# The kv products of a later batch in one run of 48 instead of two runs of 24

## Chip, cores, metric

The kernel runs on one core of a Trainium2 chip. The metric is device time in microseconds (us). Every profile holds one execution and is some 1.8 us shorter than the time of that execution, because it counts from the first to the last instruction.

## The reference

```python
def _attn_ref(q, k, v, g_norm):            # q, k, v: 8 batches, 8 heads, 576 tokens, 64
    kv = np.einsum('bhsd,bhse->bhde', k, v)     # one 64x64 matrix per head
    out = np.einsum('bhsd,bhde->bhse', q, kv)
    rms = np.sqrt(np.mean(out * out, axis=-1, keepdims=True) + 1e-06)
    return (out / rms * g_norm).astype(np.float32)

def _moe_ref(x, w_a, w_b, w_out):          # x: 4608 x 512, d_ff = 1536
    a = x @ w_a
    b = x @ w_b
    return (a * b @ w_out).astype(np.float32)
```

The attention output, with heads side by side, is the `x` of the second part. The kernel works in bf16 with float32 accumulation.

## The kernel before

The 4608 tokens are nine strips of 512. A strip has 12 "units", each with four products with `wa_t` and four with `wb_t` (128x128 weights, 512 columns), then four groups of 12 products with `wo_t`. Into strip s = 1 to 6 the attention of batch s + 1 is woven: `slot` runs after each unit n.

```python
def kv(self, p, o):                        # one pair of heads: 12 small products
    for c in range(EC):                    # EC = 6
        for j in range(2):
            nc.tensor.matmul(
                o[j * D : (j + 1) * D, :],                     # 64 partitions of the output
                lhsT=kt[self.b % NB][:, 2 * p + j, c, :],      # weights: 96 rows x 64 columns
                rhs=vt[self.b % NB][:, 2 * p + j, c, :],       # 64 columns to stream
                start=(c == 0), stop=(c == EC - 1))

def kv_out(self, src):                     # two casts, PSUM to SBUF, on ScalarE
    for j in range(2):
        r = slice(j * D, (j + 1) * D)
        nc.scalar.copy(kvb[self.b % 2][r, :, r], src[r])

def slot(A, s, n):
    kb = P[:, 7, 0 : NP * D].rearrange("q (p e) -> q p e", e=D)       # NP = 4
    k0, kn, xs = (4, 1, (6, 9, 11, 13)) if s < 3 else (1, 2, (4, 7, 10, 12))
    if k0 <= n < k0 + kn:
        for p in range((n - k0) * NP // kn, (n - k0 + 1) * NP // kn):
            A.kv(p, kb[:, p, :])
        if n == k0 + kn - 1:
            A.kv_out(kb)
    for p in range(NP):
        if n == xs[p]:
            A.x(p, X[0])          # two products, 128x128 weights, 288 columns
            A.psq(p, X[0])
        # ... (one unit later: two products with `ones`, reciprocal root, scaling)

for s in range(1, N_STRIP - 1):
    # ...
    for n in range(FC + 4):
        # ... (a unit, or from n = 12 on a group of output products)
        if A:
            slot(A, s, n)
        # ... (at n = 8: transpose and loads for later batches)
```

A "run" below is a stretch of small products between two 512-column products. Batches 2 and 3 (strips 1 and 2) already have one run of 48. Batches 4 to 7 (strips 3 to 6) have two runs of 24, after units 1 and 2.

## Time and profile before

| | before |
|---|---|
| time, median of three fast runs | 325.0 us (324.96 to 325.02) |
| the profiled run | 854.88 us, slow |
| TensorE busy in that profile | 98% |
| 512-column product, mean distance of starts there | 587 ns |

The profiled run was in another state than the timed ones. These are lines of its page: the span, the busy time of each engine, the chain of waits by engine, and two groups (busy us and mean ns of one after the first bar).

```profile
span 853.1 us, 4818 instructions
...
PE 835.1 (98%) x1922; PEld 267.5 (31%) x1957; DVE 124.7 (15%) x215; ACT 126.0 (15%) x212; POOL 60.4 (7%) x82
...
PE 96%; issue 2%; DMA 1%; POOL 0%; DVE 0%; ACT 0%; POOLq 0%
...
L234 PE MATMUL P<-xt,wb_t 128*128 128x512 bf16 x422 | 279.8, 834 | 3.4 <-issue 3.4
...
L250 DVE TENSOR_TENSOR ab<-P,asb 128x512 bf16<-128x512 f32 x108 | 74.7, 692 | 493.6 <-PE P L234 481.3
```

TensorE is busy throughout, and the chain is 96% TensorE. The next lines are the TensorE timeline of the same profile around the two runs of strip 5 (start, us from the first start to the last end, engine, line, operation, output and inputs, shapes, count).

```profile
497.00 2.65 PE L234 MATMUL P<-xt,wa_t 128*128 128x512 bf16 x4
499.35 2.65 PE L234 MATMUL P<-xt,wb_t 128*128 128x512 bf16 x4
501.92 0.94 PE L137 MATMUL P<-vt,kt 96*64 96x64 bf16 x24
502.80 0.68 PE L234 MATMUL P<-xt,wa_t 128*128 128x512 bf16 x1
503.80 1.41 PE L234 MATMUL P<-xt,wa_t 128*128 128x512 bf16 x2 [0.32 <-issue]
505.04 2.65 PE L234 MATMUL P<-xt,wb_t 128*128 128x512 bf16 x4
507.62 0.95 PE L137 MATMUL P<-vt,kt 96*64 96x64 bf16 x24
508.50 2.41 PE L234 MATMUL P<-xt,wa_t 128*128 128x512 bf16 x4
510.74 2.65 PE L234 MATMUL P<-xt,wb_t 128*128 128x512 bf16 x4
513.09 0.79 PE L234 MATMUL P<-xt,wa_t 128*128 128x512 bf16 x1
```

Reading it: starts are what to count, not ends, since products overlap. The step from 510.74 to 513.09 is 2.35 us for four products, 587 ns each. The group at 502.80 shows one product and the next two: one of four records is missing. From 497.00, where unit 1 begins, to 513.09, where unit 4 does, it is 16.09 us. Three plain units of 4.763 us take 14.29, so two runs of 24 cost 1.80 us here. The 48-product runs of strips 1 and 2 cost 1.726 us by the same count.

### The profile page before, as it was taken

The page shows a single profiled execution, that of the slowest core. Times are in us where ns is not written, and L with a number is a line of the kernel's source. Part 1 is how long each engine was busy: PE and PEld are TensorE (multiplying, and loading weights), DVE is VectorE, ACT ScalarE, POOL GpSimd, SP SyncE. Part 2 cuts the span into 40 slices and gives each one's busy share as a digit, 9 for nine tenths or more (in the row PEclk, how much of TensorE's full clock was granted, in tenths as well). Part 3 has the DMA queues.
Part 4 walks back from the last instruction along what each step waited for, and adds up shares of the span by engine and source line. Part 5 has one row for each costly group of instructions (what it writes and reads, how often), then busy time and mean ns, then how long its engine had stood idle before and what let it go on. Part 6 is the DMA issues. An engine that isn't in the chain of part 4 may idle for free.

```text
span 853.1 us, 4818 instructions
## 1 busy us (share of the span) xinstructions
PE 835.1 (98%) x1922; PEld 267.5 (31%) x1957; DVE 124.7 (15%) x215; ACT 126.0 (15%) x212; POOL 60.4 (7%) x82
## 2 busy tenths in 40 slices
PE   9999999999999999999999999999999999999998
PEld 3222333333233333333333333333333322222323
DVE  2211111111112011111111101110111011101110
ACT  2211111110122012111121011210211111001100
POOL 7610001000220020000200000000000000000000
DMA  9990028001990063002800010000000000010001
GB/s 190 197 106 0 25 53 84 0 0 38 124 111 0 25 79 57 0 13 65 85 0 0 38 40 1 0 25 26 0 0 13 37 0 0 13 37 0 1 12 37
DMA packets 70043, 32.61 MB, mean 38 GB/s; under 512 B 43652, under 2 KB 65540, under 8 KB 70020
## 3 DMA queue, kind: packets, MB, share of 16 engines
q0 software_dynamic: 49712, 18.44, 18.3%
q1 hardware_dynamic: 19952, 13.50, 5.9%
q10 hardware_dynamic: 356, 0.36, 0.2%
q8 instruction: 15, 0.25, 0.1%
q14 instruction: 8, 0.07, 0.0%
HBM read 37.75 MB, written 12.98 MB: 59 GB/s over the span
## 4 chain that ended last, share of the span: by engine, by line
PE 96%; issue 2%; DMA 1%; POOL 0%; DVE 0%; ACT 0%; POOLq 0%
PE P L234 59%; PE P L278 30%; PE P L188 3%; PE P L214 2%; PE P L137 2%; DMA qt<-in_q_dram 1%; DMA wb_t<-in_moe_w_b_dram 1%; PE P L175 1%; PE P L161 0%; PE P L303 0%; POOL wa_t L331 0%; POOL vt L96 0%; DVE osb L473 0%; POOL ident masks.py:199 0%; ACT osb L471 0%
## 5 line engine op out<-in xcount | busy, mean ns | idle before, releaser
L234 PE MATMUL P<-xt,wb_t 128*128 128x512 bf16 x422 | 279.8, 834 | 3.4 <-issue 3.4
L234 PE MATMUL P<-xt,wa_t 128*128 128x512 bf16 x419 | 277.6, 834 | 5.2 <-issue 5.2
L278 PE MATMUL P<-wo_t,ab 128*128 128x512 bf16 (+1 forms) x434 | 258.9, 817 | 3.6 <-issue 3.6
L250 DVE TENSOR_TENSOR ab<-P,asb 128x512 bf16<-128x512 f32 x108 | 74.7, 692 | 493.6 <-PE P L234 481.3
L234 PEld LDWEIGHTS <-wb_t 128*128 128x128 bf16 x432 | 73.9, 171 | 181.6 <-issue 181.1
L278 PEld LDWEIGHTS <-ab 128*128 128x128 bf16 x444 | 77.0, 174 | 166.1 <-issue 163.2
L234 PEld LDWEIGHTS <-wa_t 128*128 128x128 bf16 x432 | 74.7, 175 | 156.0 <-issue 155.2
L248 ACT CAST asb<-P 128x512 bf16<-128x512 f32 x108 | 63.2, 585 | 344.7 <-PE P L234 340.6
L202 DVE SCALAR_TENSOR_TENSOR xt<-P,g_col,rs 128x288 bf16<-128x288 f32 x64 | 30.2, 513 | 67.0 <-ACT rs L192 67.0
L192 ACT ACTIVATE rs<-P,eps_t 128x576 f32<-128x576 f32 (+1 forms) x33 | 24.0, 726 | 89.9 <-PE P L188 82.6
L291 ACT COPY osb<-P 128x512 f32<-128x512 f32 x17 | 9.9, 585 | 157.2 <-PE P L278 157.2
L184 ACT ACTIVATE sq<-P 128x576 bf16<-128x576 f32 x31 | 20.2, 650 | 81.2 <-PE P L214 72.6
L293 DVE COPY osb<-P 128x512 f32<-128x512 f32 x18 | 12.4, 691 | 132.5 <-PE P L278 132.5
L188 PE MATMUL P<-sq,ones 128*128 128x288 bf16 x64 | 29.8, 582 | 0.0
L116 POOL COPY gate<-qT 1x1 bf16<-1x1 bf16 x5 | 0.9, 176 | 337.9 <-DMA qT<-qs 337.9
L214 PE MATMUL P<-qT,kvb 128*128 128x288 bf16 x48 | 21.9, 579 | 0.0
L119 POOL DMA_DIRECT2D qs<-in_q_dram x12 | 19.6, 1633 | 1.8 <-issue 1.7
L188 PEld LDWEIGHTS <-ones 128*128 128x128 bf16 x64 | 11.2, 175 | 24.7 <-issue 24.7
L137 PEld LDWEIGHTS <-kt 96*64 96x64 bf16 x384 | 14.3, 169 | 14.5 <-issue 14.0
L137 PE MATMUL P<-vt,kt 96*64 96x64 bf16 x384 | 16.1, 262 | 0.9 <-DMA wb_t<-in_moe_w_b_dram 0.5
L214 PEld LDWEIGHTS <-kvb 128*128 128x128 bf16 x48 | 8.8, 183 | 19.9 <-issue 19.9
L303 PE MATMUL P<-zeros 128*128 128x512 bf16 x21 | 13.2, 773 | 1.2 <-DVE eps_t L318 1.2
(43 smaller groups left out, 78.3 us busy)
## 6 DMA issues: line engine op xcount, KB each, us to landing
out_dram<-osb SPq DMA_DIRECT2D x23, 256.0 KB, 2.0
qs<-in_q_dram POOLq DMA_DIRECT2D x12, 288.0 KB, 6.5
kt<-in_k_dram POOLq DMA_DIRECT2D x6, 576.0 KB, 9.0
vt<-in_v_dram POOLq DMA_DIRECT2D x6, 576.0 KB, 11.2
out_dram<-osb SPq DMA_DIRECT2D x13, 128.0 KB, 2.3
wo_t<-in_moe_w_out_dram POOLq DMA_DIRECT2D x12, 128.0 KB, 6.0
wa_t<-in_moe_w_a_dram POOLq DMA_DIRECT2D x5, 256.0 KB, 9.0
wb_t<-in_moe_w_b_dram POOLq DMA_DIRECT2D x5, 256.0 KB, 9.6
```

Source lines behind the costliest of these rows:

```text
L119: nc.gpsimd.dma_start(out=d[:, hs, :], in_=q[b, hs].rearrange("h t d -> t h d"))
L137: nc.tensor.matmul(o[j * D : (j + 1) * D, :], lhsT=kt[self.b % NB][:, 2 * p + j, c, :], rhs=vt[self.b % NB][:, 2 * p + j, c, :], start=(c ...
L184: nc.scalar.activation(sq[p % 3], P[:, i0 : i0 + 2, 0:HF], AF.Square)
L188: nc.tensor.matmul(P[:, i0 + h, 0:HF], lhsT=ones, rhs=sq[p % 3][:, h, :], start=True, stop=True)
L192: nc.scalar.activation(rs[p % 3][:, h0:h1, :], P[:, i0 + h0 : i0 + h1, 0:HF], AF.Abs_reciprocal_sqrt, bias=eps_t,)
L202: nc.vector.scalar_tensor_tensor(out=xt[p][:, t0 : t0 + HF], in0=P[:, x0 + h, 0:HF], scalar=g_col, in1=rs[p % 3][:, h, :], op0=ALU.mult, o ...
L214: nc.tensor.matmul(P[:, i0 + h, 0:HF], lhsT=kvb[self.b % 2][:, p, :], rhs=self.qT[:, p, h * HF : (h + 1) * HF], start=True, stop=True,)
L234: nc.tensor.matmul(self.a if w is wa_t else self.b, lhsT=w[:, kc, self.fc * 128 : (self.fc + 1) * 128], rhs=xt[kc][:, t0 : t0 + STRIP], st ...
L248: nc.scalar.copy(self.t, self.a)
L250: nc.vector.tensor_mul(abt[self.s % 2][self.fc], self.b, self.t)
L278: nc.tensor.matmul(P[:, i, e0:e1], lhsT=abt[s % 2][fc][:, g * 128 : (g + 1) * 128], rhs=wo_t[:, fc, e0:e1], start=(fc == 0), stop=(fc == F ...
L303: nc.tensor.matmul(P[:, i, 0:cols], lhsT=zeros[:, 0:128], rhs=zeros[:, 0:cols], start=True, stop=True)
```

## The change

The intent is to enter and leave the small products once per batch instead of twice, at equal work.

```diff
-        k0, kn, xs = (4, 1, (6, 9, 11, 13)) if s < 3 else (1, 2, (4, 7, 10, 12))
+        k0, kn, xs = (4, 1, (6, 9, 11, 13)) if s < 3 else (2, 1, (4, 7, 10, 12))
```

For strips 3 to 6 all four head pairs now run after unit 2. Nothing else moves on any engine.

## The prediction

> **What bounds it now.** TensorE. The page gives PE busy 98% of the span, DVE 15%, ACT 15%, POOL 7%; the chain of waits is 96% PE, and two lines alone, the a/b products and the output products, hold 89% of it. But the profiled run took 853 us against 325 us timed. In the timeline a 128x512 product starts every 587 ns on average (485, 621, 621, 621), while DVE and ACT instructions look normal (0.69 us and 0.59 us for 128x512). So only TensorE is slow in this profile, although its granted clock reads 1.00, and PE durations cannot be carried over one to one. The Trainium skill (TensorE: Matmul & The Clock Gate, Back-to-back issue gap) gives 215.7 ns for N=512 at full clock; the trace does not show that state. Estimate with it: 1296 such products (432 each with wa, wb and wo) take 279.5 us. With the smaller products and about 11 us of start-up, little of 325 us is left for stalls: the timed run is TensorE-bound too.
>
> **What the change does.** For batches 4 to 7 (strips 3 to 6) the 48 kv products (96x64 by 96x64) ran as 24 after unit 1 and 24 after unit 2; now all 48 follow unit 2. Instruction counts, the two kvb casts (0.37 us each, still after unit 2), loads and the x products' positions (from unit 4) are unchanged. Removed: four entries into and exits out of a run of small products. Nothing is added.
>
> **Cost of a run, from the raw order of starts.** Plain units take 4.763 us on average.
> - Batches 2 and 3 already have one run of 48: the two units around it take 11.253 and 11.252 us, 1.726 us more than two plain ones.
> - Batches 4 to 7 have two runs of 24: the three units around them take 16.084, 16.083, 16.089, 16.094 us, 1.80 us more than three plain ones.
>
> So one run instead of two saves about 0.07 us per batch in this slow state, 0.28 us in all; the products themselves cost about 36 ns each however grouped. At full clock the saving may differ. The skill (TensorEngine Tiling (Array Packing), Key Properties) says that changing the tiling mode drains TensorE. The slow trace shows little of such a drain, 34 to 68 ns a run; I allow 0.03 to 0.25 us per removed run, 0.1 to 1.0 us in all. All of it lies on the critical path.
>
> **Waits that could eat it.** The casts have unit 3 to hide behind before unit 4's x, as before. Bank 7 was last read for unit 13 of the strip before. k and v of batch 4 land at 232.9 and 236.7 us, 21 us after the transpose before them was issued; a strip in the timed run takes about 35 us, so they are early.
>
> **Prediction:** 324.6 us, 80% range 323.9 to 325.1. Faster by over 2%: 0.01; within 2%: 0.98; slower by over 2%: 0.01.
>
> **Right or wrong in the profile.** Right: the same instruction counts per line; one group of 48 kv products in strips 3 to 6; if it is again the slow state, units 1 to 3 together 16.0 us rather than 16.09; x products not preceded by idle PE. Wrong: PE idle before or after the run of 48, or a unit after it that waits for the a-copy or the multiply.
>
> **What would make it wrong.** A full-clock boundary cost far from the slow state's; a clock that reacts to a longer stretch of small products; 48 small products outrunning instruction supply and so costing more each than 24.

## The result

| | before | after |
|---|---|---|
| median, us | 325.01 (324.96 to 325.46, 4 runs) | 323.93 (323.9 to 324.1, 4 runs) |
| ratio after/before | | 0.9965, 95% interval 0.9947 to 0.9982 |

A ratio is the mean time of one kernel's fast runs over that of the other's of the same rounds, so it is not quite the ratio of the medians.

The time lies inside the stated range, at its lower end. The stated gain of 0.4 us was too small: 1.08 us was measured by the medians. The mechanism has to be checked, and its size explained.

This time the profiled run was fast. "At full clock" below means this fast state, with 216 ns a 512-column product, and "slow state" the one above, with 587 ns. These are names only: the granted clock is 1.00 in both, so what makes the slow state slow is not shown. The page after, with the same lines as before:

```profile
span 322.1 us, 4818 instructions
...
PE 314.1 (97%) x1922; PEld 151.0 (47%) x1957; DVE 124.3 (39%) x215; ACT 124.7 (39%) x212; POOL 60.3 (19%) x82
...
PE 87%; DMA 9%; POOL 1%; issue 1%; DVE 0%; ACT 0%; POOLq 0%; ACTq 0%
...
L250 DVE TENSOR_TENSOR ab<-P,asb 128x512 bf16<-128x512 f32 x108 | 74.5, 692 | 124.0 <-PE P L234 123.1
...
L234 PE MATMUL P<-xt,wb_t 128*128 128x512 bf16 x417 | 109.7, 379 | 0.4
```

VectorE's multiply still takes 692 ns; the duration of a 512-column product fell from 834 to 379 ns. So the two pages cannot be compared line by line: most of their difference is the state, not the change. The timeline after, around the run of strip 4:

```profile
157.57 1.03 PE L234 MATMUL P<-xt,wa_t 128*128 128x512 bf16 x4
158.43 1.03 PE L234 MATMUL P<-xt,wb_t 128*128 128x512 bf16 x4
159.39 0.95 PE L137 MATMUL P<-vt,kt 96*64 96x64 bf16 x48
160.27 1.04 PE L234 MATMUL P<-xt,wa_t 128*128 128x512 bf16 x3
161.15 1.03 PE L234 MATMUL P<-xt,wb_t 128*128 128x512 bf16 x4
```

Four 512-column products take 0.86 us (157.57 to 158.43), 216 ns each. The run begins 0.96 us after the four products before it began, that is 309 ns instead of 216 after the last of them: 93 ns to enter. The 48 products then start two at a time, a pair every 32 ns in the raw starts (53 ns after the first pair), so 16 ns a product. On the way out, the raw starts show 128 ns from the last kv product to the first 512-column product. From that one to the second it is 226 instead of 216 ns; here the record of the second is missing, and the 226 is read in other runs, such as the second one of strip 4 in the next profile of before. The weight loads of the same stretch show what is special at the two edges:

```profile
158.22 0.74 PEld L234 LDWEIGHTS <-wb_t 128*128 128x128 bf16 x4
159.39 0.84 PEld L137 LDWEIGHTS <-kt 96*64 96x64 bf16 x48 [0.42 <-issue]
160.27 0.55 PEld L234 LDWEIGHTS <-wa_t 128*128 128x128 bf16 x4
```

Ordinary weight loads start 2 ns after the start of the product before theirs, while it still streams. The first kv load starts at 159.39, together with its own product, and the engine's load side was idle for 0.42 us before it. The first `wa_t` load after the run, at 160.27, also starts only with its product. At both edges the load-ahead stops. The page reports no idle TensorE here, because the ends of products are modelled; the loss shows in the starts alone.

By this trace unit 2 with its run takes 2.701 us, the unit after it 1.737 and a plain one 1.727. So a run of 48 costs 2.701 + 1.737 - 2 x 1.727 = 0.984 us. Of that, 48 x 16 ns = 0.768 us is products and 0.216 us is the two edges. Four runs saved would be worth about 0.87 us at full clock, not 0.28.

### The profile page after: what moved, and what is told of

It is laid out like the page before. It is cut to its first block, busy times and chain, and to the rows that moved or that the text cites. A ratio compares the mean times of both kernels' runs of the same rounds, so it can differ in the third digit from the quotient of the medians.

```text
span 322.1 us, 4818 instructions
## 1 busy us (share of the span) xinstructions
PE 314.1 (97%) x1922; PEld 151.0 (47%) x1957; DVE 124.3 (39%) x215; ACT 124.7 (39%) x212; POOL 60.3 (19%) x82
## 4 chain that ended last, share of the span: by engine, by line
PE 87%; DMA 9%; POOL 1%; issue 1%; DVE 0%; ACT 0%; POOLq 0%; ACTq 0%
PE P L234 52%; PE P L278 28%; DMA wa_t<-in_moe_w_a_dram 5%; PE P L188 2%; PE P L214 2%; PE P L137 2%; DMA qt<-in_q_dram 2%; DMA wo_t<-in_moe_w_out_dram 1%; DMA out_dram<-osb 1%; PE P L161 0%; PE P L175 0%; POOL wb_t L108 0%; POOL wa_t L107 0%; POOL wa_t L331 0%; DVE osb L293 0%
## 5 line engine op out<-in xcount | busy, mean ns | idle before, releaser
L234 PE MATMUL P<-xt,wa_t 128*128 128x512 bf16 x425 | 111.4, 379 | 1.0 <-DVE xt L202 0.3
L234 PE MATMUL P<-xt,wb_t 128*128 128x512 bf16 x417 | 109.7, 379 | 0.4
L278 PE MATMUL P<-wo_t,ab 128*128 128x512 bf16 (+1 forms) x433 | 97.0, 373 | 0.8 <-issue 0.3
L234 PEld LDWEIGHTS <-wb_t 128*128 128x128 bf16 x432 | 42.2, 98 | 51.2 <-DMA wb_t<-in_moe_w_b_dram 0.3
L278 PEld LDWEIGHTS <-ab 128*128 128x128 bf16 x444 | 43.0, 98 | 45.8 <-issue 0.2
L234 PEld LDWEIGHTS <-wa_t 128*128 128x128 bf16 x432 | 41.7, 98 | 44.5 <-DMA wa_t<-in_moe_w_a_dram 0.3
L188 PE MATMUL P<-sq,ones 128*128 128x288 bf16 x64 | 13.2, 286 | 0.0
L214 PE MATMUL P<-qT,kvb 128*128 128x288 bf16 x48 | 10.0, 286 | 0.0
L96 POOL DMA_DIRECT2D vt<-in_v_dram x13 | 9.1, 702 | 1.1 <-DMA wo_t<-in_moe_w_out_dram 0.7
L96 POOL DMA_DIRECT2D kt<-in_k_dram x13 | 9.2, 709 | 0.0
```

Of the source, the lines that this page charges most:

```text
L96: nc.gpsimd.dma_start(out=t[:, hs, :, :], in_=src[b, hs].rearrange("h (t c) d -> t h c d", c=EC))
L188: nc.tensor.matmul(P[:, i0 + h, 0:HF], lhsT=ones, rhs=sq[p % 3][:, h, :], start=True, stop=True)
L214: nc.tensor.matmul(P[:, i0 + h, 0:HF], lhsT=kvb[self.b % 2][:, p, :], rhs=self.qT[:, p, h * HF : (h + 1) * HF], start=True, stop=True,)
L234: nc.tensor.matmul(self.a if w is wa_t else self.b, lhsT=w[:, kc, self.fc * 128 : (self.fc + 1) * 128], rhs=xt[kc][:, t0 : t0 + STRIP], st ...
L278: nc.tensor.matmul(P[:, i, e0:e1], lhsT=abt[s % 2][fc][:, g * 128 : (g + 1) * 128], rhs=wo_t[:, fc, e0:e1], start=(fc == 0), stop=(fc == F ...
```

## The experiments

Theory A: at full clock each run has a fixed cost of about 0.22 us, whatever its length. Rivals: B, only the place after unit 1 was dear; C, the saving per run is really the 0.07 us of the slow state and the rest came from elsewhere; D, small products are dear one by one, without a fixed cost.

The timed runs scatter by half a microsecond, as large as the effect of two runs, so profiles were used as well. The table gives, for the fast profiles, how much later than in the profile after each kernel reached a point: its first kv product, then the last weight load of the output products of strips 0 to 6, and under "end" that of strip 8, the last. All numbers are us, worked out from the traces. The step between two columns is what a strip costs more than in the profile after.

| kernel | first kv | strip 0 | strip 1 | strip 2 | strip 3 | strip 4 | strip 5 | strip 6 | end |
|---|---|---|---|---|---|---|---|---|---|
| before, again | 0.042 | 0.042 | 0.042 | 0.041 | 0.266 | 0.490 | 0.715 | 0.940 | 0.940 |
| one run, after unit 1 | 0.462 | 0.460 | 0.459 | 0.457 | 0.457 | 0.457 | 0.457 | 0.457 | 0.457 |
| three runs | 0.003 | -0.001 | -0.003 | -0.005 | 0.444 | 0.892 | 1.342 | 1.792 | 1.791 |
| split early | 0.666 | 0.663 | 0.886 | 1.110 | 1.109 | 1.109 | 1.109 | 1.110 | 1.110 |
| extra pair apart | 0.123 | 0.122 | 0.121 | 0.122 | 0.379 | 0.634 | 0.890 | 1.146 | 1.146 |
| extra full apart | 0.002 | 0.085 | 0.084 | 0.085 | 0.143 | 0.201 | 0.260 | 0.319 | 0.319 |
| columns only | 0.278 | 0.275 | 0.275 | 0.273 | 0.531 | 0.787 | 1.042 | 1.298 | 1.299 |
| rows only | 0.020 | 0.020 | 0.020 | 0.018 | 0.287 | 0.554 | 0.821 | 1.089 | 1.090 |
| two batches at once | 0.035 | 0.032 | 0.032 | 0.029 | 0.029 | 0.789 | -0.195 | -0.195 | -0.194 |
| after, again | 0.260 | 0.259 | 0.259 | 0.259 | 0.259 | 0.258 | 0.259 | 0.259 | 0.259 |

Outside the strips that an edit touches, columns repeat within 0.01 us, except one step of 0.08 us in strip 0. So what differs between executions is when the first useful product starts, 0 to 0.67 us here, and what an edit costs can be read from the steps.

### before_again

No edit.

> The kernel before once more, as a null control and to get its profile at full clock (the profile of before was in the slow state). Theory A: every run of small 96x64 products costs a fixed time at full clock, read from the profile after as 0.093 us on entry (309 ns from the last 512-column product to the first kv product, in place of 216) plus 0.122 us on exit, about 0.22 us. A expects: ratio 1.000; in the profile each run of 24 costs 24 x 16 ns + 0.22 us = 0.60 us over plain units, two runs 1.20 us against the 0.985 us of the one run of 48 after. Rival B: only the place after unit 1 is expensive (something there waits); then the first run of 24 shows an idle gap and the second does not. Rival C: the saving is only the 0.07 us a run of the slow state; then the rest of the measured 1.08 us lies elsewhere in the strip.

Measured: 324.81 us (324.80 to 325.04, 5 runs), ratio 0.9991 (0.9979 to 1.0004), a null as it should be. Its profile was fast. TensorE timeline of strip 4, to be held against the one after:

```profile
156.11 1.03 PE L234 MATMUL P<-xt,wa_t 128*128 128x512 bf16 x4
156.97 1.03 PE L234 MATMUL P<-xt,wb_t 128*128 128x512 bf16 x4
157.93 0.57 PE L137 MATMUL P<-vt,kt 96*64 96x64 bf16 x24
158.43 1.04 PE L234 MATMUL P<-xt,wa_t 128*128 128x512 bf16 x3
159.31 1.03 PE L234 MATMUL P<-xt,wb_t 128*128 128x512 bf16 x4
160.26 0.57 PE L137 MATMUL P<-vt,kt 96*64 96x64 bf16 x24
160.76 0.60 PE L234 MATMUL P<-xt,wa_t 128*128 128x512 bf16 x2
```

Both runs look alike: 0.95 to 0.96 us from the start of the four products before to the run, then 0.50 us to the next 512-column product. Neither has a wait. The table shows 0.225 us more than after in each of strips 3, 4, 5 and 6 and nothing elsewhere. Four times 0.225 is 0.90 us, and the lowest times differ by 324.80 - 323.90 = 0.90 us. A holds; B and C fail.

### one_run_unit1

```diff
-  ... if s < 3 else (2, 1, (4, 7, 10, 12))
+  ... if s < 3 else (1, 1, (4, 7, 10, 12))
```

> All 48 kv products of batches 4 to 7 in one run, but after unit 1 instead of unit 2. A: the number of runs counts, not the place: 323.9 us, the same as after (within 0.2 us), ratio to before 0.9965. B: the cost sits after unit 1: 324.5 to 325.0 us, little or nothing gained against before.

Measured: 323.91 us (323.90 to 324.37, 5 runs), ratio 0.9967 (0.9954 to 0.9979). The profile began 0.46 us late and lost nothing after that. The place does not matter; the number of runs does. B fails.

### three_runs

```diff
-        k0, kn, xs = ... else (2, 1, (4, 7, 10, 12))
-        if k0 <= n < k0 + kn:
-            for p in range((n - k0) * NP // kn, (n - k0 + 1) * NP // kn):
+        xs = (6, 9, 11, 13) if s < 3 else (4, 7, 10, 12)
+        runs = {4: (0, 1, 2, 3)} if s < 3 else {0: (0,), 1: (1,), 2: (2, 3)}
+        if n in runs:
+            for p in runs[n]:
                 A.kv(p, kb[:, p, :])
-            if n == k0 + kn - 1:
+            if n == max(runs):
                 A.kv_out(kb)
```

(Against the kernel after, as are all edits below.)

> Three runs (12, 12 and 24 products, after units 0, 1 and 2) for batches 4 to 7 in place of the two of before: four runs more. A with 0.22 us a run: 325.0 + 0.9 = 325.9 us, ratio 1.0027; with the 0.27 us a run that the measured change implies (1.08 us over four runs): 326.1 us, ratio 1.0033. C: at most 325.3 us. B: 325.0 to 325.3 us, unless the place after unit 0 costs too.

Measured: 326.12 us (325.68 to 326.39, 5 runs), ratio 1.003 (1.0016 to 1.0043). Each strip is 0.449 us longer than after, twice 0.225, although the runs are of 12, 12 and 24 products. The cost is per run and not per length, as A says.

### split_early

```diff
-  k0, kn, xs = (4, 1, (6, 9, 11, 13)) if s < 3 else (2, 1, ...
+  k0, kn, xs = (3, 2, (6, 9, 11, 13)) if s < 3 else (2, 1, ...
```

> Batches 4 to 7 as after (one run), but batches 2 and 3 split in two runs of 24 (after units 3 and 4): two runs more than after, two fewer than before. A: 323.93 + 2 x 0.22 to 0.27 = 324.4 to 324.5 us, ratio to before 0.998. B: 323.9 us, as the places are others. C: 323.9 to 324.1 us.

Measured: 324.97 us (324.77 to 325.14, 5 runs), ratio 0.9995 (0.9982 to 1.0007). By the time alone this missed A's 324.4 to 324.5 us. The profile says why its own run was long: it started 0.67 us late; then strips 1 and 2 took 0.223 and 0.224 us more, and strips 3 to 6 nothing. So the effect is A's in other strips too, and the time was blurred by the start. The starts of the four unprofiled runs are not known.

### extra_pair_apart

```diff
+        if s >= 3 and n == 3:
+            for j in range(2):
+                nc.tensor.matmul(
+                    P[j * D : (j + 1) * D, 7, 384 : 384 + D],     # never read
+                    lhsT=kt[A.b % NB][:, j, 0, :],                # 96 x 64
+                    rhs=vt[A.b % NB][:, j, 0, :],
+                    start=True, stop=True)
```

> The kernel after, plus two 96x64-weight products of 64 columns (into an unread corner of bank 7) on their own after unit 3 of strips 3 to 6: four added runs of the smallest size. A (fixed cost of a run, 0.217 us, plus 16 ns a product): unit 3 grows from 1.727 to about 1.98 us; the whole by 4 x 0.25 = 1.0 us, to 324.9 us with an undisturbed start. Rival D (no fixed cost; the first products of a run or each product is just dear): two products can add at most a few tens of ns each, under 0.1 us a strip, under 324.3 us.

Measured: 325.03 us (324.95 to 325.54, 4 runs), ratio 1.0004 (0.9989 to 1.0019). Two products of 64 columns in each of four strips cost what the whole change had gained. Its timeline (line 431 is the pair):

```profile
127.24 1.03 PE L234 MATMUL P<-xt,wb_t 128*128 128x512 bf16 x4
128.20 0.22 PE L431 MATMUL P<-vt,kt 96*64 96x64 bf16 x2
128.35 1.04 PE L234 MATMUL P<-xt,wa_t 128*128 128x512 bf16 x4
```

From 127.24 to 128.35 it is 1.11 us, where four plain products take 0.86. The steps in the table are 0.255 to 0.257 us a strip (0.122 to 0.379, and so on): 0.225 for the run and 0.032 for the pair. D fails.

### extra_pair_joined and pair_joined_mended

The same pair at n == 2, right behind the 48.

> The same two added products, but appended to the run of 48 after unit 2: same work as the kernel with the pair apart, no added run. A: 4 x 2 x 16 ns = 0.13 us more than after, 324.03 us; the unit with the run grows from 2.701 to 2.733 us. D: the same time as with the pair apart.

Measured: 328.3 us (328.17 to 328.79, 4 runs), ratio 1.0104 (1.0089 to 1.0119). Neither theory's number. The timeline shows a mistake of the experiment:

```profile
125.40 0.95 PE L137 MATMUL P<-vt,kt 96*64 96x64 bf16 x48
127.18 0.22 PE L431 MATMUL P<-vt,kt 96*64 96x64 bf16 x2 [0.84 <-ACT kvb L148]
127.33 1.04 PE L234 MATMUL P<-xt,wa_t 128*128 128x512 bf16 x3
```

The pair was written behind the two casts of `kv_out` and waited for them: idle 0.84 us, released by the cast to `kvb`, which reads the bank that the pair writes. Each strip became 1.058 us longer. The mended form writes the pair ahead of `kv_out`.

> The joined pair again, but written ahead of the two kvb casts, so that it doesn't wait for them: in the first form the pair started 0.84 us after the run, released by the cast of kvb, and the kernel took 328.3 us. A: the unit with the run grows from 2.701 to 2.733 us, 323.90 + 4 x 0.032 = 324.03 us with an undisturbed start. D (each added product is dear wherever it stands): 2.97 us and 325.0 us, as with the pair apart.

Measured: the three fast runs took 324.03, 324.19 and 324.37 us, ratio 0.9971 (0.9951 to 0.9990). The lowest is A's 324.03; even the highest is below the 324.95 of the pair apart. Appended to a run, the same two products cost next to nothing. The profiled execution was in the slow state (855.09 us), so the growth of the unit at full clock is not read from a trace. But this slow profile answers another question, as it can be held against the slow one of before:

```profile
504.20 2.65 PE L234 MATMUL P<-xt,wb_t 128*128 128x512 bf16 x4
506.78 1.93 PE L137 MATMUL P<-vt,kt 96*64 96x64 bf16 x48
508.42 0.33 PE L429 MATMUL P<-vt,kt 96*64 96x64 bf16 x2
508.67 0.69 PE L234 MATMUL P<-xt,wa_t 128*128 128x512 bf16 x1
```

One run with 50 products here, two runs with 24 each in the slow profile before: from one strip's run to that of the next it is 92.94 us here (413.84 to 506.78), and 92.91 us before (409.01 to 501.92); the spans are 853.3 and 853.1 us. Eight more products at the 36 ns of the prediction are some 0.29 us, or 0.07 us a strip. Three of the four strips grew by only 0.02 to 0.03 us, one by 0.16, and the span by 0.2. So in the slow state a removed run saved about 0.02 to 0.05 us. This is blurred, since the distances there are either 621 or 485 ns, 136 ns apart. At full clock the same kernel is 0.80 us faster than before, by the lowest times of the same chip (324.83 - 324.03). So a removed run was worth little in the slow state, if anything less than the 0.07 us read before the change, and 0.225 us in the other.

### extra_full_apart, cols_apart and rows_apart

The pair apart again, with weights of another shape: 128x128, then 128 rows x 64 columns, then 64 rows x 128 columns (all from `wa_t`, 64 columns to stream). The expectations call weights of 64 columns "column tiling" and weights of 64 rows "row tiling"; each is a "tiling mode", a part of TensorE's array in use instead of all of it.

> The pair apart again, with 128x128 weights and 64 columns (no column tiling) in place of 96x64 weights. If the fixed cost belongs to the change of the weights' shape (A1: the tiling mode), it vanishes: unit 3 grows only by two products of 64 columns, [...]4 x 0.1 us = 0.4 us at most, 324.3 us or less. If it belongs to any break in the stream of 512-column products (A2), unit 3 grows by about 0.25 to 0.3 us as with the small pair, 325.0 us.

Measured: 324.20 us (324.15 to 324.82, 4 runs), ratio 0.9981 (0.9964 to 0.9997).

```profile
127.20 1.03 PE L234 MATMUL P<-xt,wb_t 128*128 128x512 bf16 x4
128.07 0.22 PE L431 MATMUL P<-wa_t 128*128 128x64 bf16 x2
128.13 1.03 PE L234 MATMUL P<-xt,wa_t 128*128 128x512 bf16 x4
```

From 127.20 to 128.13 it is 0.93 us, against 0.86 for four products alone. The steps are 0.058 us a strip, which is two products of 29 ns and no fixed cost. A mere break in the stream of 512-column products is free (A2 fails); the change of the weights' shape is what costs. The kernel's own `x` products say the same: with 128x128 weights and 288 columns their starts are 122 or 123 ns apart, and the 512-column product behind them starts 121 to 123 ns after the last.

> The pair apart after unit 3, with weights of 128 rows x 64 columns: column tiling alone. If the width of the weights in columns makes the fixed cost: unit 3 and 4 grow by 0.266 us as with 96x64, 325.0 us. If the 96 rows made it: 0.058 us as with 128x128, 324.15 us.

Measured: 324.96 us (324.86 to 325.20, 4 runs), ratio 0.9995 (0.9981 to 1.0012); steps of 0.255 to 0.258 us, as with 96x64. The 96 rows are not the cause.

> The pair apart after unit 3, with weights of 64 rows x 128 columns: row tiling alone. If any change of the tiling mode makes the fixed cost: 0.27 us a strip, 325.0 us. If column tiling alone does: 0.06 us, 324.15 us.

Measured: 324.99 us (324.97 to 325.46, 4 runs), ratio 0.9998 (0.9981 to 1.0016); steps of 0.268 us. Its timeline:

```profile
127.14 1.03 PE L234 MATMUL P<-xt,wb_t 128*128 128x512 bf16 x4
128.10 0.23 PE L431 MATMUL P<-wa_t 64*128 64x64 bf16 x2
128.26 1.04 PE L234 MATMUL P<-xt,wa_t 128*128 128x512 bf16 x4
```

From 127.14 to 128.26 it is 1.12 us instead of 0.86. The two products start 39 ns apart in the raw starts, so some 0.08 us of the 0.268 is theirs and 0.19 us is the edges. Half the rows cost nearly as much as half the columns. So the fixed cost belongs to a product that uses part of the array, between products that use all of it. Slower weight loads of small weights are not the reason: the 64x128 loads take 92 to 96 ns and the 128x128 loads 98. The Trainium skill gives a reason that fits (TensorEngine Tiling (Array Packing), Key Properties: "Changing tiling mode (not just tile) drains the TensorE"). These runs agree in direction and give the size that the page does not: 0.19 to 0.225 us for entering and leaving. Whether the time goes into such a drain or into the load-ahead that stops, the traces do not separate; they show both at each edge.

### two_batches

A candidate: k and v of batch 6 have landed by strip 4, so its 48 products can follow those of batch 5 at once.

```diff
-        if k0 <= n < k0 + kn:
-            for p in range((n - k0) * NP // kn, (n - k0 + 1) * NP // kn):
-                A.kv(p, kb[:, p, :])
-            if n == k0 + kn - 1:
-                A.kv_out(kb)
+        if n == k0 and s != 5:
+            for i, a in enumerate((A, Attn(A.b + 1)) if s == 4 else (A,)):
+                kb = P[:, 7, i * NP * D : (i + 1) * NP * D].rearrange(...)
+                for p in range(NP):
+                    a.kv(p, kb[:, p, :])
+            # ... (then kv_out of each)
```

> A candidate: the kv products of batches 5 and 6 in one run of 96 after unit 2 of strip 4 (k and v of batch 6 landed 7 us before that strip begins in the profile after), both halves of bank 7, none in strip 5. One run less. A: 0.22 us less than after, 323.7 us with an undisturbed start; strips 4 and 5 together 0.217 us shorter in the profile. If k and v of batch 6 or the four casts come late, an idle gap before x and a longer time than after.

Measured: 323.69 us (323.68 to 324.06, 4 runs), ratio to before 0.9962 (0.9947 to 0.9977), and correct.

```profile
158.46 1.03 PE L234 MATMUL P<-xt,wb_t 128*128 128x512 bf16 x4
159.42 1.71 PE L137 MATMUL P<-vt,kt 96*64 96x64 bf16 x96
161.06 1.04 PE L234 MATMUL P<-xt,wa_t 128*128 128x512 bf16 x3
```

The 96 products take 1.64 us from the first of them to the next 512-column product. Strip 4 grows by 0.760 us and strip 5 shrinks by 0.984: 0.224 us gained, as for any run removed. Lowest time to lowest time it is 323.68 against 323.90 us. It beats both kernels, by 0.07% of the time after; the intervals of the ratios to before (0.9962 and 0.9965) do not separate the two, the traces do.

### after_again

No edit.

> The kernel after once more, on this chip, as a control for the start-up: until now profiles differ only by when the first useful product starts (5.78 to 6.0 us, then 7.15 to 7.82 us at the first kv product), and every later time repeats within 0.01 us. 323.9 us, or 324.1 to 324.5 us when the first loads come late; strips 3 to 6 as in the profile after to 0.01 us.

Measured: 324.14 us (323.92 to 324.21, 4 runs), ratio 0.9967 (0.9947 to 0.9986). Its profile began 0.26 us late and then ran as the first one, to 0.002 us. The control holds.

## Why the prediction was right or wrong

- **TensorE bounds the timed run: right.** At full clock TensorE is busy 97% of the span, and every step in TensorE's order of work appears in the end time.
- **The estimate of 215.7 ns for a 512-column product: right.** It came from the Trainium skill (TensorE: Matmul & The Clock Gate). The measured 215.7 stands in its section "Wait — 56ns, not 53.3ns?"; the section that the prediction names, Back-to-back issue gap, has the formula, which gives 215.8. The fast traces show 215 or 216 ns.
- **What is removed, four entries and exits, nothing added, no new wait: right.** The weight loads, casts and x products are the same in number, and no edge of the run shows an engine waited for.
- **The slow-state arithmetic, 0.07 us a run: small, as measured there, but not confirmed.** By the slow profile of the mended pair it was rather 0.02 to 0.05 us, blurred by distances that differ by 136 ns.
- **The failed step** is "The slow trace shows little of such a drain, 34 to 68 ns a run; I allow 0.03 to 0.25 us per removed run", with a central value near 0.1 us. The mechanism was right; this term was mis-sized. It measures 0.225 us a removed run at full clock, 0.90 us in four strips, where 0.4 us in all was forecast. The allowance was wide enough to hold 0.225; the central value was taken near the slow state's number, which did not carry over. So the time inside the range owes more to the width of the allowance than to the estimate.
- **Why the slow state shows less.** In the slow timeline the first 512-column product after the second run is followed by the next after about 381 ns, where 587 is the average. Over the four products this gives back some 0.1 us. It is in the lines shown: 508.50 to 510.74 is 2.24 us for four products that otherwise take 2.35. In the fast trace the same distance is 226 ns against 216, and nothing comes back. Small products cost 36 ns each there and 16 ns at full clock. This would fit a limit on throughput that the idle time of an edge did not use up, but that is argued, not shown. What holds TensorE back there stays open; the profile's granted clock reads 1.00.
- **The rest of the measured 1.08 us.** 0.90 us is the runs. Some 0.2 us lies outside strips 3 to 6. Starts that scatter by up to 0.67 us would cover it, and later runs of before reach 324.80 us. But the runs of the first comparison have no fast profile of before, so this part is argued, not shown.

## What to carry to other kernels

Products whose weights fill only half of TensorE's rows or columns belong together: each run of them among full-array products cost 0.19 to 0.225 us here, however short, while a small 96x64 product within a run cost 16 ns. Look for such runs that can be joined across heads, and, if the data has landed, across batches. And don't take a fixed cost from a profile of another state: where a profile runs 2.6 times slower than the timed runs, read order and waits from it, but get one at the right rate before sizing an effect of tenths of a microsecond.

## What the Trainium skill lacked or had wrong

- TensorEngine Tiling (Array Packing), Key Properties, says that a change of tiling mode drains TensorE but gives no size. Measured: 0.225 us for entering and leaving 96x64 or 128x64 weights, about 0.19 us for 64x128 (0.268 less two products that start 39 ns apart), none for 128x128 weights with 64 columns.
- TensorE: Matmul & The Clock Gate, What happens when you issue a matmul, describes weight loads pulled ahead of running products. The traces agree within one mode (a load starts 2 ns after the start of the product before) and show that it stops at a change of mode: the first small load starts 308 ns after the start of the last 512-column product, 92 ns after the next product would ordinarily have started.
- TensorE: Matmul & The Clock Gate, Back-to-back issue gap, gives 131 ns a product as sustained for 512 columns in a real kernel. Here weight load and product alternate and the distance is 215 or 216 ns, which is the same section's figure for an isolated product.
- TensorE: Matmul & The Clock Gate, Part 1, gives 427 ns for 512 columns at the cold clock, 216 at the warm one, a third state at 13/16 of that, a remark on a clock seen stuck at 1/4, and one on cold products that averaged 617 ns instead of 426 in one of two runs of a kernel. The fast traces agree with the first two (426 or 427 ns between the first dummy products, then 216). The two slow profiles fit none of the clocks: 587 ns on average, in steps of 485 and 621 ns, with a granted clock of 1.00 in the record. The 617 ns are close to the longer step, but the page tells of them as a matter of warm-up, and here the state lasted all 853 us.
- The same part says that the moment of warm-up varies by run, by about 0.5 us to either side, and that the whole ramp costs under 1% of a typical kernel's span. Here it varied by more: dummy products go from 427 to 216 ns apart at about 4.0 us in the profile of the 128x128 pair apart, at 5.0 us in the profile after and only after 7.0 us in that of the split in strips 1 and 2. The first kv product scattered by 0.67 us, which is only 0.2% of the span, but most of the 0.90 us that this change is worth. That the late starts come from late warm-up fits these traces but was not tested.
